# Ten pairs of seven block products in place of nine, and whole sums of h for the early pairs

## The chip, the cores and the metric

The kernel runs on one core of one Trainium2 chip. A core has five engines that run side by side, each through its own list of instructions: TensorE (PE in the profile; PEld is its weight load), VectorE (DVE), ScalarE (ACT), GpSimd (POOL) and SyncE (SP), which here only issues DMAs. They wait for each other through semaphores. The metric is the device time of one execution, in microseconds.

## The reference

The reference is a block-sorted attention followed by a feed-forward layer:

```python
B, H, S, D, n_blocks = 4, 8, 768, 64, 8          # block = 96
P = sinkhorn(sort_net)                            # five rounds of exp and normalising, 8 x 8 per head
k_sorted = einsum('bhij,bhjcd->bhicd', P, k_blocks)
v_sorted = einsum('bhij,bhjcd->bhicd', P, v_blocks)
attn = softmax(q_block @ k_sorted_block.T / sqrt(D))   # inside each block of 96
x = (attn @ v_sorted_block) -> [3072, 512]        # all heads of a token side by side
h = x @ w_in                                      # [3072, 2048]
g = maximum(h, 0) + alpha * minimum(h, 0)
out = g @ w_out                                   # [3072, 512], float32
```

Everything before `out` can be done with matrix products in bf16 and float32 accumulation, and is done so here.

## The kernel before

**Stages.** There are 32 groups of 96 tokens (`attention(g, prio)`, four batches of eight blocks). For every batch k and v are loaded, spread into block form (`conv_k`, `conv_v`, mostly on POOL), multiplied by the sorting matrix on PE (`prep_k`, `prep_v`) and copied out of PSUM. A group then gives scores, softmax and 96 columns of `xT`. The feed-forward layer runs beside the attention of later groups. `ffn1(tok, end, ft, prio)` makes 128 of the 2048 features of `g` for a chunk of 192 or 384 tokens: four matmuls on PE (line 889), a ReLU of the negative on ACT (line 899), and a scalar_tensor_tensor on DVE (line 903) that writes the tile `hT`. In the kernel's own names `hT` is therefore `g`, stored with features on the partitions; the text says h for it. `ffn2(t, prios)` multiplies one tile of 128 tokens by `w_out`: 16 matmuls of 512 columns (line 928), a copy to `outstg` and a store.

**Pairs.** Two neighbouring tiles can be taken together by `strassen(ta, prio)`. The tokens are halved by tile (ta, ta+1), the features by even and odd blocks of 128, the output columns by left and right 256. That is a 2 x 2 block product, and it is made with seven block products in place of eight. Each is eight matmuls of 256 columns (line 1027), added in two halves (hf 0 and 1) as two list entries. Four sums of h are needed (line 1002), n = 1 to 4, where n = 2 reads n = 1, and n = 4 reads n = 2; four of the seven products read a sum of h, the other three read `hT` itself. Before the change each sum is made in two operations of 512 columns (hf 0 covers features 0 to 1023, hf 1 the rest). `snap` copies the running sum in PSUM to SBUF three times a pair (line 414, the tile `sn` or, for every other pair, `KSz`), `total` adds it to a bank (line 1042), `store` sends the tile out. The sums of w_out that the products need are made once for all pairs, by `w_sums` (line 966): eight operations of 1024 columns, into `KS[1]`, `VST[1]` and `WT3`, buffers that hold keys and values of batch 1 and masks until then. The dictionary `PAIRS` names the first tile of each pair and which of two sets of buffers it uses.

**What sets the order.** Every operation is recorded in `_Graph` under a number, in the order in which the program adds it. The string `SEQ` is an order of all of them, written out: a bare number leaves the operation on the first engine that it may use, a letter p, a or d puts it on POOL, ACT or DVE, and an entry such as `i4H` is a run of matmuls that only keep PE busy. Each engine runs its operations in that order and waits (`wait_ge`) for what it depends on; `sums` and `w_sums` may run on DVE (the default) or POOL, copies out of PSUM on ACT (the default) or DVE. Nothing is decided when the kernel runs. All loads are issued by POOL, between its computing operations, and the stores and transposes by SP.

**Rings.** `hT` has room for 1024 tokens. `CHUNKS` says where each chunk of tokens lies, so that a chunk may be overwritten only when the tiles in it have been multiplied by w_out.

Of the kernel before, what the change touches and what calls it, by code (L numbers as in the profile page):

```python
# [48 lines left out]
460 397 474 398d 424 437d 453 475 425 477 462 478 461 516 426d 463 427 428 476 505 517 466 170 454 479 498 455
456d 467d 483 518 506 457 501 499 492 502 458d 465 500 493 464 552 484 510 511 366 503 490 371 513 553 494 512  # L50
514 519 370 373 485 491 507 554 534 515 537 508d 495d 372 369 546 581 535 486d 536 496 367 538 365 497 487 540
539 368 543 488d 555 530 541 582 531 520 544 542 583 521 547 561 647 562d 568 584 545 522d 509 548 651 569 565
570 563 566 572 573 523 549 383 550 571 564 524d 590 574 567 591 648 575 650 578 576 592 525 579 577 594 595
556 593 617 596 655 614 399 597 580 623 557 632 653p 615 558d 559 652 616 624 618 489 633 657p 626 600 560 625
585 619 429 627 634 601 586 599 629 630 628 587d 641 551 642 654 656 631 620 643 588 589 635 598 691 644 692
685 621 645 603 646 663 664 602 604 686 688 693 689 659 605 665d 694 622 700 666 701 687 658 660 708 702 690
720 667 709 703 710 661 459 711 668 712 714 721 713 715 669 704 706 722 670 716 707d 717 718 671d 705 723 737
731 738 749 732 662 719 672 750 740 673 739 741 735 730 636 743 674 675 637 638d 742 751 695 676 696 778 697d
746 677 736 744 758 779 729 678 724 759 745 752 747 748 725 679 766 780 726d 769 760 734 753 767 768 837 770
639 733 698 772 761 781 763 754 788 773 764 771 755d 848 765 775 681 838 776 774 847 762 777 682 853 789 727  # L60
795 613 683 798 787 839 801 846 796 611 799 790d 802 849 756 809 606 797 800 610 810 791 852 811 840 866 782
805 806 812 608 792 867 803 793 684 794 831 832 807 813 833 607 814 609 804 850 834 851 815 612 816 874 868
835 817d 854 818 875 855 783 784d 819 924 841 836 877 876 881 820 878 857 879 869 821 808 822 823 858 925 926
824 934 880 935 859 863 856 888 860 825 842 932 827 828 864 892 865 885 861 933 889p 862 882 829 843d 886 936
887 883 896 937d 927 893p 884 870 897 921 894p 938 680 918 922 898d 871 890 640 939 923 899 872d 952 919 920
895p 900 943 844 901d 940 944 902 941 953 903 891p 928 954 699 945 949 785 904d 942 905 906 929 966p 1002 930d
946 907 1003 950 873 947 728 908 951 931 909 948 910 911 963 960 967p 955 1004 1022 912 964 965 757 961 914
962 1023 999 968p 996 976 915 1000 997 956 786 969p 1001 998 957 1013 970p 916 1024 1010 977 1042 971p 1011
972 1005 974 975 973p 958d 1014 1012 1016 978 830 1015 1019 1025 1017 1043 913 1020 980 979 1006 981 1018 982
1021 1030 1033 1044 1031 986d 1034 983 1007 959 1008d 1026 987 1032 1035 1045 1036 1027 1148p 1028d 826 1037  # L70
1038 1039 1076p 1062 1040 984 1050 1041 1029 1009 1063 1053 1046 988 1077p 1051 1054 985 989 845 1052 1078p
917 1047 1048d 1056 1064 1084 1057 990 1055 1085 1058 1146p 992 1059 1060 1079p 1112 1088 993 1049 1065 1061
1070 994 1071 1073 1074 1072 1086 1075 1087 1113 1106 1089 1107 1109 1090 1110 1080p 1066 1108 991 1111 1092
1093 1114 1150 1120 1121 1094 1122 1115 1081p 1091 1132 1096 1123 1082p 1126 1097 1124 1098 1133 1127 1125
1129 1147p 1128 1134 1099d 995 1095 1154 1140 1083 1155 1130 1067 1100 1102 1141 1103 1131 1152p 1068 1158
1149p 1135 1182 1143 1142 1176 1160 1183 1104 1144 1156 1145 1177 1116 1157 1178 1184 1179 1210 1180 1190 1151
1117 1159 1161 1162 1153p 1191 1181 1163 1069 1193 1192 1185 1118 1196 1194 1136 1166d 1167 1197 1195 1137
1168 1169 1198 1208p 1138d 1199 1202 1200 1164 1201 1119 1165 1205 1203 1204 1238 1216 1217 1206 1207 1239
# [1165 lines left out]
```

## Time and profile before

| | us |
|---|---|
| three runs | 230.91, 234.92, 365.86 |
| their median | 234.92 |
| the execution that was profiled | 230.35 |
| its span, first to last instruction | 228.6 |
| what lies around the span | 1.75 |

The granted clock of TensorE was 1.00 over the whole span. The profile lists for each engine how long it was busy and what it waited for. Busy time of PE is the union of its instructions, and a matmul's record lasts longer than the spacing of two matmuls that follow each other closely, so small gaps between matmuls don't show as idle; the starts in the timeline show them. Numbers such as L1002 are lines of the program; line 414 is the one helper that makes all copies, so its groups are told apart by their tiles.

### The profile page before, as it was taken

Reading aid. Unit: us, or ns where it says so; the run is one execution under the profiler, and the core shown is the slowest. Engines: PE = TensorE matmul, PEld = TensorE weight load, DVE = VectorE, ACT = ScalarE, POOL = GpSimd, SP = SyncE. Lnnn points to the kernel's source line nnn. Section 1 sums busy time; section 2 is a strip of 40 time slices with the busy share of each in tenths; the row PEclk is TensorE's granted clock in tenths of the full one; section 3 lists DMA queues with packets and bytes.
Section 4 is the critical chain, followed back from the end, with each engine's and each line's share of the span. In section 5 each row is a group of like instructions: output and inputs, shape, how many; then the busy total and the mean of one; then the engine's idle time right before and its main releaser. Section 6 shows DMA issues by size and latency. Waiting matters only on the chain.

```text
span 228.6 us, 6971 instructions
## 1 busy us (share of the span) xinstructions
PE 218.5 (96%) x2807; PEld 158.1 (69%) x2807; DVE 192.3 (84%) x419; ACT 160.5 (70%) x448; POOL 152.8 (67%) x182
## 2 busy tenths in 40 slices
PE   3898999999999999999999999999999999999994
PEld 3467588685556656546677877777777777999983
DVE  5669599897898999999999999989878877878584
ACT  4378667889989987778788885567676797554310
POOL 7969129859498995992999999954385712624660
PEclk9999999999999999999999999999999999999999
DMA  5999999995994199679944995477343524040304
GB/s 65 214 214 196 215 206 193 178 178 81 187 214 97 34 152 105 140 77 212 229 91 82 136 124 124 81 100 174 92 118 81 83 52 99 3 126 3 138 3 185
DMA packets 64033, 29.05 MB, mean 127 GB/s; under 512 B 55280, under 2 KB 58880, under 8 KB 64000
## 3 DMA queue, kind: packets, MB, share of 16 engines
q0 software_dynamic: 24816, 13.63, 44.6%
q1 hardware_dynamic: 39184, 14.97, 31.9%
q8 instruction: 22, 0.36, 0.7%
q14 instruction: 11, 0.09, 0.1%
HBM read 27.28 MB, written 6.29 MB: 147 GB/s over the span
## 4 chain that ended last, share of the span: by engine, by line
PE 66%; DVE 10%; DMA 10%; POOL 9%; ACT 2%; issue 1%; POOLq 0%
PE psH L889 29%; PE psYP L1027 19%; DMA KS<-in_k_dram 10%; PE psYP L928 5%; POOL KSz L664 3%; DVE hT L903 3%; PE psS L764 3%; PE psO L818 3%; PE psYP L718 2%; PE psO L1027 2%; DVE xq L831 1%; PE psS L1027 1%; POOL w_in_bf L1105 1%; DVE VST L966 1%; POOL QN L444 1%
## 5 line engine op out<-in xcount | busy, mean ns | idle before, releaser
L889 PE MATMUL psH<-xT,w_in_bf 128*128 128x384 bf16 (+1 forms) x624 | 98.2, 295 | 0.5 <-DVE hT L903 0.3
L903 DVE SCALAR_TENSOR_TENSOR hT<-t,omaT,psH 128x384 bf16<-128x384 f32 (+1 forms) x156 | 79.7, 529 | 16.8 <-ACT t L899 15.7
L899 ACT ACTIVATE t<-psH 128x384 f32<-128x384 f32 x126 | 61.6, 496 | 34.9 <-PE psH L889 32.1
L889 PEld LDWEIGHTS psH<-xT,w_in_bf 128*128 128x128 bf16 x624 | 54.2, 98 | 21.7 <-DVE hT L903 2.3
L798 ACT ACTIVATE Esb<-psS,nf 96x96 bf16<-96x96 f32 x192 | 46.3, 346 | 0.6 <-DVE nf L770 0.6
L414 POOL COPY VDz<-VST 64x384 bf16<-64x384 bf16 x40 | 35.3, 882 | 9.4 <-PE psYP L718 3.7
L664 POOL COPY KSz<-KS 64x512 bf16<-64x512 bf16 x36 | 26.0, 721 | 16.4 <-DMA KS<-in_k_dram 11.9
L928 PE MATMUL psYP<-w_out_bf,hT 128*128 128x512 bf16 x96 | 24.3, 379 | 0.0
L770 DVE TENSOR_REDUCE nf<-psS 96x8 f32<-96x768 f32 x24 | 22.7, 948 | 1.4 <-PE psS L764 1.3
L1002 POOL TENSOR_TENSOR Sm<-hT 128x512 bf16<-128x512 bf16 x11 | 13.2, 1204 | 15.2 <-DVE hT L903 14.7
L444 POOL DMA_DIRECT2D QN<-in_q_dram x24 | 20.1, 844 | 0.0
L831 DVE TENSOR_TENSOR xq<-psO,rec 96x512 bf16<-96x512 f32 x27 | 18.4, 683 | 0.4
L1002 POOL TENSOR_TENSOR VDz<-hT 128x512 bf16<-128x512 bf16 x7 | 8.2, 1170 | 14.6 <-DVE hT L903 14.3
L1027 PE MATMUL psYP<-w_out_bf,hT 128*128 128x256 bf16 x128 | 17.9, 273 | 0.0
L1027 PEld LDWEIGHTS psYP<-w_out_bf,hT 128*128 128x128 bf16 x128 | 12.1, 98 | 2.5
L928 PEld LDWEIGHTS psYP<-w_out_bf,hT 128*128 128x128 bf16 x96 | 8.4, 97 | 7.2
L414 ACT ACTIVATE VS<-psYP 112x512 bf16<-112x512 f32 x17 | 11.8, 692 | 1.8 <-PE psYP L718 1.8
L818 PE MATMUL psO<-VS,ET 112*128 112x65 bf16 x248 | 12.7, 194 | 0.1
L818 PEld LDWEIGHTS psO<-VS,ET 112*128 112x128 bf16 x248 | 10.6, 98 | 1.8 <-DVE xq L831 0.4
L764 PEld LDWEIGHTS psS<-KT,QTz 64*128 64x128 bf16 (+1 forms) x248 | 6.5, 97 | 7.0 <-ACT t L899 2.3
L764 PE MATMUL psS<-KT,QTz 64*128 64x96 bf16 (+1 forms) x248 | 10.8, 206 | 0.4 <-DVE KT L414 0.2
L414 ACT ACTIVATE KT<-psYP 128x512 bf16<-128x512 f32 x15 | 8.9, 597 | 2.9 <-PE psYP L677 2.9
(196 smaller groups left out, 364.0 us busy)
## 6 DMA issues: line engine op xcount, KB each, us to landing
out_dram<-outstg SPq DMA_DIRECT2D x24, 256.0 KB, 2.5
KS<-in_k_dram POOLq DMA_DIRECT2D x3, 768.0 KB, 9.6
QN<-in_q_dram POOLq DMA_DIRECT2D x24, 96.0 KB, 4.5
w_in_bf<-in_moe_w_in_dram POOLq DMA_DIRECT2D x4, 512.0 KB, 18.8
w_out_bf<-in_moe_w_out_dram POOLq DMA_DIRECT2D x2, 1024.0 KB, 19.9
VST<-in_v_dram POOLq DMA_DIRECT2D x4, 384.0 KB, 10.9
hT<-in_q_dram POOLq DMA_DIRECT2D x1, 768.0 KB, 7.3
VST<-in_v_dram POOLq DMA_DIRECT2D x1, 768.0 KB, 13.2
```

Of the source, the lines that this page charges most:

```text
L414: return e.activation(o, i, ACTF.Copy) if e is nc.scalar else e.tensor_copy(o, i)
L444: G.add(POOL, lambda e, h=h: e.dma_start(AP(QN, h % 4 * 128 + h // 4 * 64, [[3072, 128], [512, 6], [1, 64]]), AP(q.tensor, b * HB + h * S ...
L664: G.add(POOL, lambda e, hp=hp: e.tensor_copy(AP(KSz, hp * 64 * 3072 + u % 3 * 1024 + hp * 64, [[3072, 64], [128, 8], [1, 64]]), AP(KS[n], ...
L764: inst = e.matmul(o, AP(QTz[n], hp * 64 * 3072 + h4 * 768 + i * 96, [[3072, 64], [1, w]]), AP(KT[n], hp * 64 * ld + (h4 * 8 + i) * bk, [[l ...
L770: G.add(DVE, lambda e: e.tensor_reduce(AP(nx, 0, [[8, 96], [4, 2], [1, 4]]), AP(psX, 0, [[1024, 96], [512, 2], [96, 4], [1, 96]]), AxisLis ...
L798: inst = e.activation(AP(Esb[me], p * 128, [[1024, 96], [64, 2], [1, 48]]), AP(psX, (p // 4) * 512 + (p % 4) * 96, [[1024, 96], [48, 2], [ ...
L818: inst = e.matmul(AP(psZ, hp * 512 + h4 * 68, [[1024, 128], [1, 65]]), AP(ET[me] if far else ET[m], pos(h4, hp) * 96, [[800, nk], [1, 128] ...
L889: inst = e.matmul(AP(pt, poff + x * n, [[1024, 128], [1, n]]), AP(w_in_bf, kt * DFF + (ft + x) * 128, [[KT_TILES * DFF, 128], [1, 128]]), ...
L899: G.add(ACT, lambda e: e.activation(AP(t1, tb, [[1152, 128], [1, k * n]]), AP(pt, poff, [[1024, 128], [1, k * n]]), ACTF.Relu, scale=-1.0) ...
L903: G.add(DVE, lambda e, x=x: e.scalar_tensor_tensor(out=AP(hT, (ft + x) * RING + place(tok), [[FT_TILES * RING, 128], [1, n]]), in0=AP(t1, ...
L928: inst = e.matmul(AP(bank[0], bank[1], [[1024, 128], [1, n]]), AP(hT, ft * RING + place(tok), [[FT_TILES * RING, 128], [1, 128]]), AP(w_ou ...
L1027: inst = e.matmul(AP(pt, po + off, [[1024, 128], [1, 256]]), sa, mb, start=begin and j == 0, stop=j == 7, skip_group_check=True)
```

## The change

There are three parts.

- In `strassen`, pairs whose first tile is below 20 take each sum of h in one operation over all 1024 columns (eight feature blocks of 128 in place of four), and it waits for all 16 feature blocks of `hT`. Pairs 20 and 22 keep two operations of 512.
- `PAIRS` gets the entry `4: 0`: tiles 4 and 5, until now two calls of `ffn2`, become a tenth pair. Since `w_sums` is called ahead of the first pair, its operations are recorded ahead of pair 4.
- `SEQ` is another order from its 372nd entry on (about 60 us into the span). The numbers shift as well, since 14 fewer operations are recorded (1348 for 1362).

```diff
@@ -42,48 +42,47 @@
 270 264d 279 299 286 284 165 267 287 265 300 162 266d 277 273 289 280 274d 306 288 334 166 275 335 301 276 293
...
-344d 357 329 358 349 388 377 408 319 389 390 409 411 391 249 330 168 412 410 392 413 347 414 415 331 348d 351
-352 649 332 416 417 420 346d 418 526 527 438 421 350d 353 164p 533 439 360 361 419 532 354d 528 441 400 440
...
+344d 357 329 358 349 388 377 408 319 389 390 409 411 391 249 330 168 412 410 392 413 347 526 393 414 348d 331
+415 350d 351 420 532 346d 416 417 169 352 332 418 421 438 419 360 529 439 353 440 354d 422 441 546p 548 442
...
@@ -391,7 +390,7 @@
...
-    PAIRS = {6: 0, 8: 0, 10: 0, 12: 1, 14: 0, 16: 1, 18: 0, 20: 1, 22: 0}
+    PAIRS = {4: 0, 6: 0, 8: 0, 10: 0, 12: 1, 14: 0, 16: 1, 18: 0, 20: 1, 22: 0}
...
@@ -985,22 +984,27 @@
         def hk(t, odd, hf):
             return [("hT", 8 * hf + 2 * j + odd, y) for j in range(4) for y in gr[t]]
 
+        whole = ta < 20
+        nj = 8 if whole else 4
+
         def blk(t, odd, hf):
-            return AP(hT, (8 * hf + odd) * RING + (ra, rb)[t], [[FT_TILES * RING, 128], [2 * RING, 4], [1, 128]])
+            return AP(hT, (8 * hf + odd) * RING + (ra, rb)[t], [[FT_TILES * RING, 128], [2 * RING, nj], [1, 128]])
 
         def sv(n, hf):
-            return AP(st, (n - 1) * 1024 + hf * 512, [[ld, 128], [128, 4], [1, 128]])
-        for hf in range(2):
+            return AP(st, (n - 1) * 1024 + hf * 512, [[ld, 128], [128, nj], [1, 128]])
+        for hf in range(1 if whole else 2):
+            hfs = (0, 1) if whole else (hf,)
             for n, x, y, op in ((1, (1, 0), (1, 1), AluOpType.add), (2, 1, (0, 0), AluOpType.subtract),
                                 (3, (0, 0), (1, 0), AluOpType.subtract), (4, (0, 1), 2, AluOpType.subtract)):
                 r = []
                 for v in (x, y):
-                    r += [("S", m, v, hf)] if isinstance(v, int) else hk(*v, hf)
+                    for z in hfs:
+                        r += [("S", m, v, z)] if isinstance(v, int) else hk(*v, z)
...
-                G.add(SMALL, f, {"dve": 520, "pool": 1180}, r=r, w=[("S", m, n, hf)] + first, prio=prio + n / 100)
+                G.add(SMALL, f, {"dve": 90 * nj, "pool": 270 * nj}, r=r, w=[("S", m, n, z) for z in hfs] + first, prio=prio + n / 100)
```

Read through the numbering of operations, the new lists place the 48 sums of h as follows. On DVE: 20 whole ones and 9 halves. On POOL: 12 whole ones and 7 halves. The old lists had 33 halves on DVE and 39 on POOL. Of the eight sums of w_out two are now on POOL (one before). Of the copies of `VS` out of PSUM 3 go from DVE to ACT, of those of `KT` one.

More of the change, by code (lines that the diff above doesn't have):

```diff
@@ L49 @@
[L49 to L78, printed above, removed]
@@ new lines @@
+803 840 804 639 858 811 837 812 817 813 856 841 873 838 818 846 839 857 814 819 859 792 880 793 820 634 821
+822 881 823d 636 638 884 860 874 824 794d 825 847 842 637 635 861 885 640 926 882 826 863 827 690 828 927 862
+864 575 829 830 865 831 869 875 883 894 848 866 886 833 834 928 934 870 871 867 891 868 935 694 887 888 929
+849d 835 892 889 876 938 893 939 898 899 890 936 937 900d 877 662 895 923 940 738 924 941 920 901 896p 902 954
+921 925 945 795 709 878d 922 942 946 903d 943 955 947 904 905 956 930 906d 951 907 908 944 1000 948 952 931
@@ new lines @@
+932d 909 1001 910 911 912 796 953 913 949 850 897 950 879 1002 965 962 1020 966 974 933 963 914 957 967 964
+997 994 1003 916 998 836 1021 995 851 999 917 1022 958 996 1011 918 832 959 1008 968p 975 1009 1012 969 1040
+970 972 767 960 973 1010 1014 1023 1013 971 976 1017 1015 1004 1041 977 1018 1016 978 979 1042 980 1019 1028
+1031 961 1029 1060 1032 981 1005 1006d 984d 1030 1033 1024 1061 1034 1035 1037 1025 1043 982 985 919 1038 1036
+986 1062 1007 1039 983 1051 1052 1026d 1027 987d 988 1048 1053 1044 1045 1063 990 991 1049 1057 1050 1054
@@ new lines @@
+1046d 1106 1078 992 1058 1059 1071 1055 1056 1047 1072 1068 1080 1107 1079 1069 1073 1108 1070 1082d 1064 1074
+1081 1100 1083 1103 1075 1101 1104 1126 1102 1086 1084 1114 1115 1105 993 1117 1118 1065 1116 1085 1087 1090
+1076p 1120 1119 1109 1121 1123 915 1091 1124 1066d 1127 1088 1110 1142p 1089 1122 1111 1077p 1125 1128 1092
+1093d 1134 1094 1137 1135 1172 1136 1096 1138 1166 1139 1140p 1173 1167 1097 1168 1141p 1169 1170 1067 1174
+1129 1144 1145 1098 1148d 1171 1146 1180 1147 1112d 1113 989 1183 1150 1181 1182 1184 1151 1185 1156d 1186
@@ L87 @@
+1213 1302 1270 1273 1299 1300 1303 1301 1201p 1261p 1306 1304 1328 1334 1218 1271 1305 1307 1308 1310 1309
+1165 1311 1259 1320 1263 1276 1312 1318 1314 1315 1316 1220 1277 1319 1221 1317 1274 1313 1326 1322 1327 1330
+1222 1335 1278 1332 1275 1279 1323 1280 1333 1338d 1336 1329 1223 1282 1324p 1339 1340 1337 1341 1219 1283
+1321p 1342 1284 1343 1266 1267 1269 1344 1325p 1345 1331 1281 1346 1285 1347
 """.split()
```

30 lines of the change are left out of this document (20 added, 10 removed).

## The prediction

> **What bounds the kernel now.** I read the busy times first, then a table of four stages.
>
> ```profile
> PE 218.5 (96%) x2807; PEld 158.1 (69%) x2807; DVE 192.3 (84%) x419; ACT 160.5 (70%) x448; POOL 152.8 (67%) x182
> ...
> 0.00:55.00 55.00, 48.80 (x1053) 36.16 (x1054) 43.47 (x125) 38.58 (x76) 38.14 (x58) 1.00 1.15 174
> 55.00:105.00 50.00, 49.54 (x521) 28.96 (x520) 45.59 (x80) 41.94 (x124) 41.23 (x51) 1.00 0.92 131
> 105.00:215.00 110.00, 109.78 (x1142) 84.07 (x1141) 94.89 (x196) 78.61 (x246) 68.56 (x70) 1.00 0.59 106
> 215.00:228.60 13.60, 10.38 (x98) 8.95 (x95) 8.33 (x19) 1.37 (x3) 4.85 (x5) 1.00 0.26 98
> ```
>
> The columns of the table are the stretch, its length, then busy time and instructions of PE, PEld, DVE, ACT, POOL, then granted clock and DMA. From 55 to 215 us PE is idle for 0.7 us of 160. It is the bound wherever the change acts; the first 55 us run by the part of the lists that stays as it is. The view of waits agrees. PE's longest wait is at the start, and behind the start nothing holds it for more than half a microsecond in total:
>
> ```profile
> PE psYP L1201 <- ACT identb L414: 3.1, 1, 3.1
> ...
> PE psYP L677 <- POOL KSz L664: 0.5, 2, 0.3
> ```
>
> Busy time hides small gaps, because the record of a matmul overlaps the next one. So I took prices from starts in the timeline of PE (start, duration, instruction):
>
> ```profile
> 67.63 0.41 PE L818 MATMUL psO<-VS,ET 112*128 112x65 bf16 x8
> 67.87 1.03 PE L928 MATMUL psYP<-w_out_bf,hT 128*128 128x512 bf16 x4
> 68.74 0.40 PE L718 MATMUL psYP<-BDV,VDz 128*128 128x64 bf16 x8
> 68.97 0.81 PE L889 MATMUL psH<-xT,w_in_bf 128*128 128x384 bf16 x4
> 69.62 0.34 PE L853 MATMUL psO<-identb,xq 96*128 96x96 bf16 x4
> 69.79 1.03 PE L928 MATMUL psYP<-w_out_bf,hT 128*128 128x512 bf16 x4
> 70.75 0.34 PE L764 MATMUL psS<-KT,QTz 64*128 64x96 bf16 x8
> 71.03 0.82 PE L889 MATMUL psH<-xT,w_in_bf 128*128 128x384 bf16 x4
> ```
>
> Start to start, four matmuls of 512 columns take 0.87 us, four of 384 take 0.65, eight of the attention 0.23 to 0.28, four transposes 0.17. The stretch 55 to 105 holds these:
>
> ```profile
> L889 PE MATMUL psH<-xT,w_in_bf 128*128 128x384 bf16 x128 | 25.0, 326 | 0.2
> L928 PE MATMUL psYP<-w_out_bf,hT 128*128 128x512 bf16 x80 | 20.2, 379 | 0.0
> L718 PE MATMUL psYP<-BDV,VDz 128*128 128x64 bf16 x96 | 4.8, 193 | 0.0
> L818 PE MATMUL psO<-VS,ET 112*128 112x65 bf16 x64 | 3.3, 194 | 0.0
> L764 PE MATMUL psS<-KT,QTz 64*128 64x96 bf16 x62 | 2.7, 205 | 0.0
> L853 PE MATMUL psO<-identb,xq 96*128 96x96 bf16 x32 | 2.7, 206 | 0.0
> L677 PE MATMUL psYP<-BDM,KSz 128*128 128x64 bf16 x48 | 2.4, 193 | 0.2 <-POOL KSz L664 0.2
> L764 PE MATMUL psS<-KT,QTz 64*96 64x96 bf16 x10 | 0.6, 212 | 0.0
> ```
>
> 32 x 0.65 + 20 x 0.87 + 18 x 0.23 + 8 x 0.24 + 9 x 0.28 + 8 x 0.17 = 48.1 us of 50. Gaps of 1.9 us in this stretch are therefore the most that a better order could win there, apart from less work.
>
> **Part one, tiles 4 and 5 as a pair.** Removed from PE are 2 x 16 matmuls of 512 columns: 8 groups of four at 0.87 = 6.96 us. Added are 7 x 8 of 256 columns. Their price is in the chain of waits:
>
> ```profile
> 134.17 1.75 PE psYP L1027 x16
> ```
>
> 1.75 / 16 = 0.109 us, times 56 = 6.13 us. PE gains 0.83 us, and as PE is the bound, I count all of it. The pair puts work on other engines: four sums, three snaps, three totals, less two copies to the staging tile.
>
> **Part two, whole sums.** The durations of the halves, by engine (12 groups, 33 on DVE and 39 on POOL; here the first of each engine), and of the nearest operations of 1024 columns, the sums of w_out:
>
> ```profile
> L1002 DVE TENSOR_TENSOR Sm<-hT x13: 366/418/581, 94.9 to 219.8; 128x512 bf16<-128x512 bf16 x13
> L1002 POOL TENSOR_TENSOR Sm<-hT x11: 1152/1157/1479, 98.1 to 218.0; 128x512 bf16<-128x512 bf16 x11
> ...
> L966 DVE TENSOR_TENSOR WT<-w_out_bf x2: 681/682/682, 60.8 to 93.6; 128x1024 bf16<-128x1024 bf16 x2
> L966 DVE TENSOR_TENSOR VST<-w_out_bf,KS x2: 677/1344/2010, 91.1 to 96.6; 128x1024 bf16<-128x1024 bf16 x2
> L966 POOL TENSOR_TENSOR KS<-w_out_bf,VST x1: 2118/2118/2118, 95.9 to 95.9; 128x1024 bf16<-128x1024 bf16 x1
> ```
>
> A whole sum is between 0.68 us and two halves, 0.84, on DVE; I take 0.68, the row of its own size. On POOL it is between 2.12 and 2.31; I take 2.12 for the same reason. Undisturbed, sums on POOL go from 39 x 1.157 = 45.1 us to 12 x 2.12 + 7 x 1.157 = 33.5, and on DVE from 33 x 0.418 = 13.8 to 20 x 0.68 + 9 x 0.418 = 17.4. The other operations that the lists move are priced by these rows:
>
> ```profile
> L1042 DVE TENSOR_TENSOR outstg<-psYP,sn 128x256 f32<-128x256 f32 x10 | 4.1, 414 | 0.6 <-PE psYP L1027 0.6
> L1042 DVE TENSOR_TENSOR outstg<-psYP,sn 128x512 f32<-128x512 f32 x5 | 3.4, 670 | 0.7 <-PE psYP L1027 0.7
> L414 DVE COPY sn<-psYP 128x256 f32<-128x256 f32 x8 | 3.4, 420 | 0.6 <-PE psYP L1027 0.6
> L414 DVE CAST VS<-psYP 112x512 bf16<-112x512 f32 x9 | 6.2, 685 | 0.0
> L414 ACT ACTIVATE VS<-psYP 112x512 bf16<-112x512 f32 x17 | 11.8, 692 | 1.8 <-PE psYP L718 1.8
> ```
>
> DVE gets 3.6 for sums, 1.5 for totals and 0.4 for one snap; it loses three copies of VS, one of KT and one output copy (0.69 each) and a sum of w_out (0.68), 4.1 together: 193.7 us, 1.4 more. ACT gets the four copies (2.8 by its own row) and two snaps for one output copy: about 163.5. POOL loses 11.6 and gets one sum of w_out: 143.3. None of them exceeds PE's load, so on the average all of it lies beside PE, and POOL's relief is worth nothing by itself. The cover is thinnest in 55:105, where DVE already has 45.6 of 50 us; there it gets the pair's four sums, totals and two snaps (5.0) and gives back four copies out of PSUM (2.8), the w_out sum, and the two halves of pair 6 that start before 105 (0.8). That is 46.3 of the 49.2 that remain, so PE still covers it. If the cover fails, each further microsecond of DVE is one of the kernel; that is the second rival.
>
> Waiting for all 16 feature blocks in place of eight makes a sum start later. Queued behind a waiting sum on DVE are the `hT` writes that free PE's banks for `ffn1`. In the new lists the sums stand behind the last `ffn1` of their chunk, and PE gets the products that read `hT` itself first; I cost this at nothing, and its bounds are the gaps: 0 to a few tenths for each of eight pairs, at most 2.
>
> **Part three, the order.** The sums of w_out move from 88 to 102 us down to some 63 to 95, and one of them, on POOL (2.1), is put ahead of `conv_v` of batch 2. POOL is idle for 8.8 of 50 us in the table's second stretch, so this fits, and the loads of batch 3 behind it on its queue should start at about the same place. The cost is taken as zero, between the 1.9 that could be won and the same lost. At the end:
>
> ```profile
> 216.25 0.66 PE psH L889 x8
> ...
> 224.73 0.89 PE psO L1027 x8
> ```
>
> Behind the last `ffn1` matmul (216.91) stood 19 half products, 8.3 of the 8.7 us until 225.6. In the new list 22 stand there, so PE has more to do while the last sums are made, and only their order changes.
>
> **Sum.** 228.6 - 0.83 = 227.8 of span, with the 1.75 around it 229.5 us. It is made against the profiled execution (230.35), which agrees with the fastest run (230.91). The median of the runs shown, 234.92, lies 4.6 above the profiled time and was not explained by any row.
>
> **Rivals.** First, the new order also closes gaps. For it speaks that gaps of 1.9 us exist in 55:105, and that copies out of PSUM, for which PE's next work waits, go from DVE to ACT; against it, that DVE gets no lighter there. At most 1.9 beside the 0.83, and an allowance of 1.0 for the gaps behind 105, which I did not count: 230.35 - 3.7 = 226.6 us.
>
> Second, slower: DVE and POOL hold each other up, and DVE becomes the bound. The timeline of the last sums shows how:
>
> ```profile
> 219.99 2.56 POOL L1002 TENSOR_TENSOR Sm<-hT,Sm 128x512 bf16<-128x512 bf16 x2 [0.88 <-DVE Sm L1002]
> 220.17 1.37 DVE L1002 TENSOR_TENSOR VDz<-hT,VDz 128x512 bf16<-128x512 bf16 x1
> ```
>
> The other long sums on DVE are these:
>
> ```profile
> L1002 DVE TENSOR_TENSOR Sm<-Sm,hT x6: 411/421/824, 102.3 to 219.5; 128x512 bf16<-128x512 bf16 x6
> L1002 DVE TENSOR_TENSOR VDz<-hT x5: 412/417/932, 155.7 to 207.2; 128x512 bf16<-128x512 bf16 x5
> ```
>
> A DVE sum of 0.42 us begun just after a POOL sum took 1.37, until that one had ended; the w_out sum of 2.01 us above lay beside POOL's of 2.12 in the same way. The Trainium skill states the rule ("SBUF — State Buffer", section "SBUF: two separate sides"): a DVE operation with two SBUF inputs and a GpSimd operation that reads SBUF take one pair of ports in turn, whichever is first for its whole instruction. Both rows agree with it. By that rule, an operation twice as long holds the other twice as long, and this speaks against whole sums. In the old run the longest of each group cost DVE (1.37 - 0.42) + (2.01 - 0.68) + (0.82 - 0.42) + (0.93 - 0.42) + (0.58 - 0.42) = 3.4 us. Doubled, that is 3.4 us more; it decides from about 2.9 us on (46.3 + 2.9 fills 49.2). If all of the holds fall where DVE is full and PE waits out each one, the time is 229.5 + 3.4 = 232.9 us. Against it: the lists leave half as many sums on POOL, and in 55:130 nearly none.
>
> Third, the pair gives PE nothing, because the 0.83 us turn into gaps ahead of products that wait for sums: 230.4 us.
>
> **Numbers.** Forecast 0.60 (its own range 228.8 to 230.2); gaps closed 0.15; DVE bound 0.15; nothing gained 0.10. The range goes down to 227.2, most of the way to the first rival, and up to 234.2, which takes in the second rival and a forecast that stands as far above its profile as the median of the runs shown does (234.92 - 0.83 = 234.1). About 2% (4.6 us) is what a measurement of this kernel can tell from no change. Faster by more than that (below 225.7) needs more than all gaps: 0.05. Slower (above 235) needs DVE's holds and a further loss, such as the loads of batch 3 starting late: 0.07. Within: 0.88.
>
> **What would show it.** Right: 64 matmuls of 512 columns for w_out in place of 96, 560 of 256 columns in place of 504, PE's busy time down by about 0.8, whole sums of 0.68 us on DVE and 2.1 on POOL, and PE idle for under 1 us from 55 to 215. Wrong on the gaps: prices and counts of the same stretch of PE come to over 49 of 50 us. Wrong on DVE: sums of 1.5 us and more between 60 and 130, DVE above 48 of 50, and PE waiting for a product's sum. It would also be wrong if the wait of POOL for batch 3's values grew well beyond what it is now.

## The result, and the profile after

The change makes the kernel slower: 237.32 us at the median against 231.5 (the median of six executions of the old kernel, in place of the three known before), a ratio of 1.0264 with a 95% interval of 1.0227 to 1.0301. The ratio leaves out the executions that lie over 1.5% above the fastest of their kernel: 239.59 us of the new, 234.92 and 365.86 us of the old. The execution that was profiled took 235.75 us with a span of 233.9, against 230.35 and 228.6: 5.3 us more of span.

The busy times of the new kernel, in the first part of its page:

```profile
PE 218.5 (93%) x2831; PEld 160.5 (69%) x2831; DVE 198.8 (85%) x413; ACT 162.4 (69%) x446; POOL 143.0 (61%) x163
```

PE is busy for as long as before, and the span is longer, so the 5.3 us are idle time of PE. The table of stretches says where. Its columns are those of the table in the prediction (stretch, length, then PE, PEld, DVE, ACT, POOL, clock, DMA). After:

```profile
55.00:105.00 50.00, 48.31 (x538) 30.66 (x536) 45.51 (x82) 43.65 (x128) 42.85 (x52) 1.00 0.85 122
105.00:170.00 65.00, 64.32 (x700) 46.97 (x699) 60.36 (x111) 52.29 (x166) 34.35 (x39) 1.00 0.88 132
170.00:180.00 10.00, 7.40 (x71) 4.70 (x68) 9.70 (x12) 4.66 (x14) 4.57 (x2) 1.00 0.43 104
180.00:210.00 30.00, 29.83 (x284) 24.30 (x285) 24.01 (x51) 17.12 (x51) 13.89 (x7) 1.00 0.31 68
210.00:220.00 10.00, 9.07 (x96) 8.32 (x95) 7.82 (x17) 3.67 (x9) 5.64 (x4) 1.00 0.04 13
```

Before, two of the same places (105 to 215 together and 55 to 105 stand in the prediction):

```profile
170.00:180.00 10.00, 10.00 (x93) 7.00 (x91) 7.46 (x13) 6.29 (x19) 6.56 (x6) 1.00 0.49 91
210.00:220.00 10.00, 10.00 (x104) 9.31 (x102) 6.75 (x19) 3.60 (x9) 4.62 (x5) 1.00 0.22 80
```

From 170 to 180 PE loses 2.60 us, from 210 to 220 0.93, and from 55 to 105 1.23 more than before (1.69 for 0.46). That is 4.8 us; the stretches from 105 to 170 (0.68 idle for 0.22) and from 180 to 210 (0.17 for none) add 0.6. From 220 us to the end PE is idle for 3.2 us in both kernels. From 170 to 180 DVE is at 9.70 of 10 with only 12 instructions. The view of waits of the new kernel, for PE (total, times, longest):

```profile
PE psH L888 <- DVE hT L902: 1.7, 4, 0.9
PE psYP L1031 <- DVE Sm L1006: 1.6, 1, 1.6
PE psYP L1031 <- DVE outstg L1046: 1.2, 1, 1.2
...
PE psYP L717 <- POOL VDz L413: 1.0, 1, 1.0
```

The lines have shifted: L888 is `ffn1`, L902 the write of `hT`, L1006 a sum of h, L1031 a block product, L1046 a total, L413 the helper of copies, L717 the product with the values, L965 a sum of w_out. Before, PE's wait for `hT` came to 0.3 us, and the others shown are not in that view.

**175 to 180 us.** The timeline of the new kernel (start, duration, instruction, and in brackets the idle time before it and what ended it):

```profile
174.92 2.12 POOL L1006 TENSOR_TENSOR Sm<-hT 128x1024 bf16<-128x1024 bf16 x1 [18.26 <-DVE hT L902]
...
175.09 2.50 DVE L1006 TENSOR_TENSOR Sm<-hT 128x1024 bf16<-128x1024 bf16 x1
...
177.12 2.44 POOL L1006 TENSOR_TENSOR VDz<-hT 128x1024 bf16<-128x1024 bf16 x1
177.51 0.41 DVE L1046 TENSOR_TENSOR outstg<-psYP,sn 128x256 f32<-128x256 f32 x1
177.84 2.27 DVE L1006 TENSOR_TENSOR Sm<-Sm,hT 128x1024 bf16<-128x1024 bf16 x1
177.98 0.61 PE L1031 MATMUL psYP<-KS,hT 128*128 128x256 bf16 x4 [1.19 <-DVE outstg L1046]
180.03 1.13 DVE L902 SCALAR_TENSOR_TENSOR hT<-t,omaT,psH 128x384 bf16<-128x384 f32 x2
180.17 0.61 PE L1031 MATMUL psYP<-VST,Sm 128*128 128x256 bf16 x4 [1.58 <-DVE Sm L1006]
```

POOL begins a sum at 174.92. DVE's sum of two tiles begins at 175.09, 0.17 us behind it, and ends at 177.59, 0.55 us after POOL's (177.04). Its undisturbed time is 0.68, so it stood still for about 1.8 us. The total queued behind it on DVE, which frees the bank that PE's next product needs, comes at 177.51. Then it happens again: POOL begins at 177.12, and DVE's next sum, begun at 177.84, takes 2.27. The total itself, which reads PSUM and one tile in SBUF, took its usual 0.41 beside POOL's sum. The bracket of the first line says how the two came to begin together: POOL had waited 18.26 us for a write of `hT`, and DVE, which makes these writes, reaches its own sum of the same pair right behind it (after one copy). In the old kernel's timeline the same stretch has POOL sums of half the size, six in a row from 174.06 to 181.4 us, and beside the first five a single DVE sum:

```profile
175.29 1.16 POOL L1002 TENSOR_TENSOR Sm<-Sm,hT 128x512 bf16<-128x512 bf16 x1
176.14 0.59 DVE L1002 TENSOR_TENSOR VDz<-hT 128x512 bf16<-128x512 bf16 x1
```

That one met POOL's too, but only the last 0.31 us of it, and cost DVE 0.17 (0.59 for 0.42).

**213 us.** One of the last `ffn1` groups waits in the same way, as the writes of `hT` that free its banks are queued on DVE behind a held sum:

```profile
213.00 2.12 POOL L1006 TENSOR_TENSOR Sm<-hT,Sm 128x1024 bf16<-128x1024 bf16 x1
...
213.32 2.07 DVE L1006 TENSOR_TENSOR VDz<-hT 128x512 bf16<-128x512 bf16 x1
...
215.32 1.38 DVE L902 SCALAR_TENSOR_TENSOR hT<-t,omaT,psH 128x192 bf16<-128x192 f32 x4
216.10 0.83 PE L888 MATMUL psH<-xT,w_in_bf 128*128 128x192 bf16 x8 [0.93 <-DVE hT L902]
```

**83 us.** This one is no sum. POOL's queue now has two conversions of keys and the product of a mask (L623) ahead of the last conversion of values of batch 2, and PE's product with these values waits:

```profile
78.31 2.25 POOL L663 COPY KSz<-KS 64x512 bf16<-64x512 bf16 x2
80.62 1.77 POOL L413 COPY VDz<-VST 64x384 bf16<-64x384 bf16 x2
82.47 0.95 POOL L623 TENSOR_TENSOR BDV<-mkhV,dsel 128x64 bf16<-128x64 f32 x1
83.49 0.82 POOL L413 COPY VDz<-VST 64x384 bf16<-64x384 bf16 x1
...
84.45 0.39 PE L717 MATMUL psYP<-BDV,VDz 128*128 128x64 bf16 x8 [1.00 <-POOL VDz L413]
```

The waits of 1.6, 1.2, 0.9 and 1.0 us at these three places add up to 4.7 us; the span grew by 5.3.

### The profile page after: what moved, and what is told of

Its sections match the earlier page's. It is cut to its first block, busy times and chain, and to the rows that moved or that the text cites. A ratio compares the mean times of both kernels' runs of the same rounds, so it can differ in the third digit from the quotient of the medians.

```text
span 233.9 us, 6983 instructions
## 1 busy us (share of the span) xinstructions
PE 218.5 (93%) x2831; PEld 160.5 (69%) x2831; DVE 198.8 (85%) x413; ACT 162.4 (69%) x446; POOL 143.0 (61%) x163
## 4 chain that ended last, share of the span: by engine, by line
PE 56%; POOL 19%; DMA 15%; DVE 5%; issue 2%; ACT 2%; POOLq 0%; DVEq 0%
PE psH L888 25%; PE psYP L1031 20%; DMA KS<-in_k_dram 13%; POOL VDz L413 7%; POOL KSz L663 5%; PE psO L1031 2%; PE psO L817 2%; PE psS L763 2%; DVE Sm L1006 2%; DMA ET<-Esb 2%; PE psS L1031 1%; DVE hT L902 1%; PE psYP L717 1%; PE psYP L676 1%; POOL w_in_bf L1109 1%
## 5 line engine op out<-in xcount | busy, mean ns | idle before, releaser
L888 PE MATMUL psH<-xT,w_in_bf 128*128 128x384 bf16 (+1 forms) x624 | 97.7, 295 | 1.7 <-DVE hT L902 1.7
L902 DVE SCALAR_TENSOR_TENSOR hT<-t,omaT,psH 128x384 bf16<-128x384 f32 (+1 forms) x156 | 79.5, 528 | 13.8 <-ACT t L898 12.0
L888 PEld LDWEIGHTS psH<-xT,w_in_bf 128*128 128x128 bf16 x624 | 54.2, 98 | 22.2 <-DVE hT L902 3.2
L797 ACT ACTIVATE Esb<-psS,nf 96x96 bf16<-96x96 f32 x192 | 46.3, 345 | 0.3 <-DVE nf L769 0.3
L413 POOL COPY VDz<-VST 64x384 bf16<-64x384 bf16 x40 | 36.1, 902 | 7.0 <-PE psYP L717 2.9
L663 POOL COPY KSz<-KS 64x512 bf16<-64x512 bf16 x36 | 23.6, 657 | 14.2 <-DMA KS<-in_k_dram 11.9
L1006 POOL TENSOR_TENSOR Sm<-hT 128x1024 bf16<-128x1024 bf16 (+1 forms) x5 | 10.1, 2022 | 34.2 <-DVE hT L902 34.1
L1006 POOL TENSOR_TENSOR VDz<-hT 128x1024 bf16<-128x1024 bf16 (+1 forms) x6 | 10.1, 1690 | 20.0 <-DVE hT L902 19.7
L1031 PE MATMUL psYP<-w_out_bf,hT 128*128 128x256 bf16 x144 | 20.0, 273 | 0.0
L830 DVE TENSOR_TENSOR xq<-psO,rec 96x512 bf16<-96x512 f32 x28 | 19.1, 681 | 0.4
L927 PE MATMUL psYP<-w_out_bf,hT 128*128 128x512 bf16 x64 | 16.1, 379 | 0.0
L1031 PEld LDWEIGHTS psYP<-w_out_bf,hT 128*128 128x128 bf16 x144 | 13.3, 98 | 2.9 <-ACT sn L413 0.2
L413 ACT ACTIVATE VS<-psYP 112x512 bf16<-112x512 f32 x20 | 13.9, 695 | 1.2 <-PE psYP L717 0.9
L717 PEld LDWEIGHTS psYP<-BDV,VDz 128*128 128x128 bf16 x192 | 8.2, 98 | 4.3 <-ACT t L898 1.4
L413 ACT ACTIVATE KT<-psYP 128x512 bf16<-128x512 f32 x16 | 9.5, 597 | 2.0 <-PE psYP L676 1.9
```

Source lines behind the costliest of these rows:

```text
L413: return e.activation(o, i, ACTF.Copy) if e is nc.scalar else e.tensor_copy(o, i)
L663: G.add(POOL, lambda e, hp=hp: e.tensor_copy(AP(KSz, hp * 64 * 3072 + u % 3 * 1024 + hp * 64, [[3072, 64], [128, 8], [1, 64]]), AP(KS[n], ...
L797: inst = e.activation(AP(Esb[me], p * 128, [[1024, 96], [64, 2], [1, 48]]), AP(psX, (p // 4) * 512 + (p % 4) * 96, [[1024, 96], [48, 2], [ ...
L888: inst = e.matmul(AP(pt, poff + x * n, [[1024, 128], [1, n]]), AP(w_in_bf, kt * DFF + (ft + x) * 128, [[KT_TILES * DFF, 128], [1, 128]]), ...
L902: G.add(DVE, lambda e, x=x: e.scalar_tensor_tensor(out=AP(hT, (ft + x) * RING + place(tok), [[FT_TILES * RING, 128], [1, n]]), in0=AP(t1, ...
L1006: return e.tensor_tensor(out=sv(n, hf), in0=i[0], in1=i[1], op=op)
```

## The experiments

The theory after this reading, **holds**: the second rival of the prediction at places that the prediction had not named. A POOL sum that begins first stops a DVE operation with two inputs in SBUF until it ends, and PE waits for what is queued behind. The rivals: **order**, the new list is laid out worse for POOL and DVE whatever their sums do; **size**, an operation of 1024 columns is the cause wherever it stands; and **pair**, the tenth pair costs more than it saves. All runs below were compared with the old kernel on the same chip (medians of 231.17 to 231.28 us). Diffs of the list show the moved entries between their neighbours, with `...` for what lies between; the text says what the entries are.

### Taking the meetings apart

In the first kernel the sum of w_out that the change put on POOL ahead of the values of batch 2 goes to DVE.

```diff
-422 441 546p 548 442
+422 441 546 548 442
```

> The changed kernel with one edit: the w_out sum n = 1, hf 0, goes from POOL back to DVE at the same place of the list. Theory 'POOL order': that 2.3 us operation delays POOL's conversions of batch 2 until PE waits 1.0 us for one of them at 84 us; the gap goes, and the span falls by about 1.0 to 1.2 us, to some 232.8. Theory 'DVE load' (DVE, busy 198.8 us, is simply too full): DVE gets 0.7 us more, the gap at 84 moves to another product, and the time stays or rises by up to 0.7. Theory 'holds only' (all of the loss is at 175 and 213 us): no change beyond 0.3 us.

238.52 us, 1.0314 [1.0269, 1.0359]: slower yet. The wait at 83 us stayed (1.0 us, now at 84), for POOL used the free time to wait for the load of the values:

```profile
64.89 14.06 POOL L413 COPY VDz<-VST 64x384 bf16<-64x384 bf16 x13 [2.78 <-DMA VST<-in_v_dram]
```

So that sum of w_out is not what delays the values, and the gain of 1.0 to 1.2 us expected for it did not come. A new loss came at 140 us, where the new kernel had none:

```profile
138.53 2.12 POOL L1006 TENSOR_TENSOR Sm<-hT 128x1024 bf16<-128x1024 bf16 x1
138.98 2.21 DVE L1006 TENSOR_TENSOR Sm<-hT 128x1024 bf16<-128x1024 bf16 x1
```

In the new kernel DVE began this sum at 138.06, 0.28 us ahead of POOL (138.34), and took 0.74; POOL took 2.44. Here POOL began 0.45 us ahead, and PE waited 1.1 us. Nothing at this place had been edited. Between the medians (238.52 for 237.32) that is about the whole difference; the profiled execution, the slowest of the four with 239.48, also ran at half clock for a while, which the end of this document takes up.

In the second kernel, pair 14's third sum (1076) goes from POOL to DVE, between the first and the second, and pair 16's third (1142), also on POOL, behind pair 14's fourth. The sums are as large and as many; only the two meetings at 175 and 177 us are gone.

```diff
-1064 1074 1081 ... 1090 1076p 1120 ... 1110 1142p 1089 ... 1111 1077p 1125
+1064 1074 1076 1081 ... 1090 1120 ... 1110 1089 ... 1111 1077p 1142p 1125
```

> The changed kernel with one edit at 175 us: the sum n = 3 of pair 14 goes from POOL to DVE, between n = 1 and n = 2, and POOL's n = 3 of pair 16 goes behind n = 4 of pair 14. So POOL runs nothing beside DVE's sums n = 1 and n = 2 of pair 14. Theory 'holds': these two take 0.68 us in place of 2.50 and 2.27, PE's gaps of 1.2 and 1.6 us there go, and the span falls by 2.5 to 3.0 us, to some 231.2. Theory 'DVE load': DVE has 0.68 us more in a stretch where it is busy for 9.7 of 10 us, so PE's gaps stay at 2.5 us or more and the span stays at 233.5 to 234.6.

233.38 us, 1.0099 [1.0084, 1.0114]. The sums that had taken 2.50 and 2.27 us now take 0.68 or less each:

```profile
175.53 1.28 DVE L1006 TENSOR_TENSOR Sm<-hT 128x1024 bf16<-128x1024 bf16 x2
...
177.07 0.68 DVE L1006 TENSOR_TENSOR Sm<-Sm,hT 128x1024 bf16<-128x1024 bf16 x1
```

POOL's next sum begins at 177.83, when they have ended. The stretches of this kernel:

```profile
170.00:180.00 10.00, 10.00 (x91) 6.54 (x89) 8.90 (x19) 5.39 (x17) 2.12 (x1) 1.00 0.42 103
210.00:220.00 10.00, 9.08 (x96) 8.28 (x95) 8.47 (x20) 3.76 (x9) 4.09 (x4) 1.00 0.01 2
```

Two entries give back 3.9 of 5.8 us of the medians, and 2.3 us of span between the profiled executions (231.6 for 233.9; *holds* expected 2.5 to 3.0, a DVE that is simply too full at most 0.4). The medians differ by more because the clock stays up as well: the mean granted clock is 0.999 or 1.000 in all four executions. PE is full from 170 to 180, with DVE at 8.90 of 10 in place of 9.70, while DVE has 19 instructions in place of 12: it does more and is busy for less. This is what *holds* says. *Size* alone and *pair* would have left the loss in place. At 210 to 220 nothing was edited and nothing changed.

In the third, all 32 whole sums are on DVE (the letter p of twelve entries is taken away; five of them are shown).

```diff
-576 671p 700 ... 1008 968p 975 ... 1090 1076p 1120 ... 1160 1198p 1099 ... 1301 1201p 1261p
+576 671 700 ... 1008 968 975 ... 1090 1076 1120 ... 1160 1198 1099 ... 1301 1201 1261p
```

> The changed kernel with all 32 whole sums on DVE at their places in the list (12 come from POOL). DVE gets 12 x 0.68 = 8.2 us and loses the holds of its sums (2.50 + 2.27 + 2.07 + 1.53 in place of 0.68 + 0.68 + 0.42 + 0.68, 5.9 us). Theory 'holds': PE's gaps at 175 to 180 and at 215 go (3.9 us in all), span about 230. Theory 'DVE load': DVE's sum of work rises above 200 us, its queue is late in more places, span 234 to 238.

235.2 us, 1.0168 [1.0146, 1.0191]. The meetings at 175 are gone, and PE is full from 170 to 180, but DVE now has too much to do behind 180 us, and PE waits there:

```profile
180.00:195.00 15.00, 13.83 (x114) 9.38 (x112) 13.24 (x25) 9.00 (x27) 0.00 (x0) 1.00 0.21 48
```

PE loses 1.2 us of 15 from 180 to 195. It also waits 1.0 us for converted values at 84 us, as in the changed kernel, and 1.0 us for converted keys at 46 us, where the lists are still those of the old kernel. The span is 233.7 us, where *holds* alone expected about 230 and a DVE that is simply too full 234 to 238; DVE is busy for 200.5 us. So once no meeting is left, DVE's load does count in this list: twelve sums moved give back less than the two entries of the second kernel.

The fourth joins the first two edits and puts pair 18's fourth sum (1201), the one of 213 us, on DVE.

```diff
-1301 1201p 1261p
+1301 1201 1261p
```

> The two edits of the first two runs together, and the whole sum n = 4 of pair 18 moved from POOL to DVE (it holds a DVE sum of pair 20 for 1.65 us at 213, and PE then waits 1.1 us). Theory 'POOL order' and 'holds' together: the span falls by 1.1 + 2.8 + 1.1 = 5.0 us to some 229, level with the kernel before or up to 0.8 us under it if the pair's saving is real; measured time about 230 to 231. Theory 'DVE load': 233 or more. If the pair costs more than it saves, the span stays 1 us or more above that of before even with these gaps gone.

234.17 us, 1.0136 [1.0116, 1.0156]. The loss at 213 us is gone, as *holds* says. The wait at 84 (1.0) and the meeting at 140 us of the first kernel (1.1) are both there, which makes it slower than the second alone. The span of 229 us that was expected from the sum of the three did not come (232.7): the edits don't add up, for an edit can shift POOL and DVE against each other behind it, as at 140 us.

### The other places

From here on the edits of the second kernel and the one of 213 us are kept. In this one a conversion of keys (528), one more (527) and the mask product (164p) go behind the conversion of values that PE waited for at 83 us.

```diff
-428 528 170 ... 498 527 499 ... 551 164p 500 ... 580 460 458
+428 170 ... 498 499 ... 551 500 ... 580 460 528 527 164p 458
```

> The changed kernel with three edits of the list: pair 14's n = 3 on DVE with POOL's n = 3 of pair 16 behind n = 4 of pair 14 (as in the second run), pair 18's n = 4 on DVE, and POOL's two key conversions and one small mask product of batches 2 and 3 moved behind the last value conversion of batch 2, which is what PE waits for at 84 us. Theory 'holds and POOL order': the span falls from 231.6 (second run) by 1.1 at 213 us and by 1.1 at 84 us, to 229.4, within 1 us of the kernel before. Theory 'POOL is simply behind from its load of values': the gap at 84 us stays at 1 us or moves to the first key product, span 230.5. Theory 'DVE load': the edit for pair 18 brings nothing, span 231 or more.

233.41 us, 1.01 [1.0054, 1.0146]; the four executions spread from 232.67 to 234.22. The wait at 83 us is gone, so it was the order of POOL's queue. But the span of 229.4 us that was expected did not come (232.2). PE now waits 0.5 us for converted keys at 93 us, and two meetings cost it 0.9 us at 99 and 1.1 at 140. The second is that of the first experiment; the first is between two sums of w_out:

```profile
96.71 2.11 POOL L965 TENSOR_TENSOR KS<-w_out_bf,VST 128x1024 bf16<-128x1024 bf16 x1
97.23 2.15 DVE L965 TENSOR_TENSOR VST<-w_out_bf,VST 128x1024 bf16<-128x1024 bf16 x1
```

The next moves one conversion of keys (528) in place of two, and takes the two meetings apart: the sum of w_out (552) and pair 12's first sum (968) go to DVE.

```diff
-498 499 ... 460 528 527 164p 458 ... 588 553 645 ... 652 552p 615d ... 1008 968p 975
+498 527 499 ... 460 528 164p 458 ... 588 553 552 645 ... 652 615d ... 1008 968 975
```

> The changed kernel with every meeting of a POOL sum and a DVE sum taken out that was seen to make PE wait: pair 14's n = 3 and pair 18's n = 4 on DVE, pair 16's n = 3 behind n = 4 of pair 14 (as in the eighth run), and also pair 12's n = 1 and both halves of the fourth w_out sum on DVE; of POOL's work ahead of the last value conversion of batch 2 only one key conversion and the mask product are moved behind it. Theory 'holds': against the run with three places (span 232.2) PE's gaps of 1.3 us at 140, of about 0.6 of the 1.0 at 99 and of 0.5 at 93 go, span 229.8, which is within 0.5 us of the kernel before in the same session (229.5). Theory 'the new order is slow for other reasons': 231.5 or more.

232.4 us, 1.0052 [1.0025, 1.0078]: the fastest form of the change, and still slower than the old kernel by 1.2 us. The losses at 83, 99, 140, 175 and 213 us are gone; seven entries of some 1350 give back 4.9 of 5.8 us. For the wait at 83 us it was *order* that was right, for the others *holds*. What is left at single places behind 65 us is a wait of 0.7 us for converted keys at 93 us and one of 0.4 for a transpose at 121.5. The span is 230.7 us, between the 229.8 that *holds* expected and the 231.5 of its rival, and 2.1 us above the old kernel's profile. Of these, 0.7 us arise ahead of 56 us, where the lists are the same (a group of `ffn2` begins at 56.12 for 55.43 us), so this one profile does not say what the difference of the medians is made of.

The last kernel takes these two. Three of the eight loads of q that POOL issues ahead of the conversions of keys (368, 369, 372) go behind the third of them, with them the first transpose of q (383), and on PE one attention product (763) goes behind the `ffn1` group (782) that followed it.

```diff
-559 368 610 ... 531 369 597 ... 589 372 562 ... 591 383 600 ... 533 584 ... 854 763 782 764
+559 610 ... 531 597 ... 589 562 ... 591 600 ... 533 368 369 372 383 584 ... 854 782 763 764
```

> Keeps all three parts and the moves of the kernel without meetings, and takes two of its three remaining gaps: the last three of the eight loads of q for batch 2 go on POOL behind three conversions of keys (the PE gap of 0.82 us at 93 us stood behind 6.7 us of load issues), and on PE one second attention product goes behind the ffn1 group that followed it (the gap of 0.59 us at 121.5 us stood for its transpose). Theory of the order (what is left of the loss is the places of single entries): both gaps close, the time falls by 1.0 to 1.4 us from that of the kernel without meetings, to a ratio of 0.999 to 1.001, so that the pair's gain is all that is left to win. Rival (what is left is the weight of the new work itself, spread over many small waits): the gaps open at the next products and the ratio stays at 1.004 to 1.006.

234.47 us, 1.0139 [1.0114, 1.0164]: slower by 2 us. Both gaps closed, and two larger ones opened, one of 1.6 us for a transpose at 97 us, the other here:

```profile
102.77 2.11 POOL L477 DMA_DIRECT2D VST<-in_v_dram  x4 [6.37 <-DMA QTz<-QN]
...
107.12 2.11 POOL L1006 TENSOR_TENSOR Sm<-hT 128x1024 bf16<-128x1024 bf16 x1
...
107.73 2.05 DVE L1006 TENSOR_TENSOR Sm<-hT 128x1024 bf16<-128x1024 bf16 x1
...
110.17 1.05 PE L1031 MATMUL psYP<-w_out_bf,hT 128*128 128x256 bf16 x8 [0.91 <-DVE outstg L1046]
```

The later loads of q make the transposes of q late. POOL then waits 6.37 us for these before it issues the loads of values, and so begins the next pair's sum at 107.12 in place of 104.67 us, 0.61 ahead of one of DVE's: a meeting where there had been none (that sum of DVE had taken 0.68), caused by entries some 15 us ahead of it. The expectation of 1.0 to 1.4 us less was wrong, and its rival named neither of these places; that the last 1.2 us are in the places of single entries is not shown.

### The parts of the change alone

Two kernels leave tiles 4 and 5 as calls of `ffn2`, everything else as in the two kernels above that they answer to (three places, and no meetings).

```diff
-    PAIRS = {4: 0, 6: 0, 8: 0, 10: 0, 12: 1, 14: 0, 16: 1, 18: 0, 20: 1, 22: 0}
+    PAIRS = {6: 0, 8: 0, 10: 0, 12: 1, 14: 0, 16: 1, 18: 0, 20: 1, 22: 0}
```

> The kernel of the run before with pair 4 taken away alone: tiles 4 and 5 again by 16 matmuls of 512 columns each, in the places of the pair's products, its sums, snaps and totals left out, all else in the same order. Theory 'the pair saves its matmuls': PE has 0.83 us more to do, and the span is 0.6 to 0.9 us longer than that of the run before. Theory 'the pair costs more than it saves' (its 5 us of DVE work between 80 and 110 us open gaps on PE): the span is the same or up to 1.5 us shorter.

> The kernel of the run before without pair 4 (tiles 4 and 5 by 512-column matmuls in the places of the pair's products). Theory 'the pair saves its matmuls': 0.6 to 0.9 us longer than the run before, since no gap hides it now. Theory 'the pair costs more than it saves': the same or shorter by up to 0.9 us, as in the earlier pair of runs (231.3 without, 232.2 with).

The first took 232.91 us, 1.0063 [1.0042, 1.0085], less than the 233.41 of its counterpart with the pair. But in it DVE began the sum at 139 us ahead of POOL (139.24 and 139.52), so that the wait of 1.1 us at 140 was missing; it doesn't measure the pair. The second has a counterpart without meetings: 232.89, 1.0072 [1.0052, 1.0092], for 232.40 with the pair. With the pair it is 0.5 us less between the medians and 0.6 of span (231.3 for 230.7); the forecast was 0.83. The intervals overlap, so the size of this saving is not shown. PE's idle time behind 55 us is about the same in the two (5.0 us with the pair, 5.2 without), though not at the same places: without the pair PE waits 0.8 us for a write of `hT` at 107 us. *Pair* falls: in the one comparison without meetings the pair costs no time.

The next undoes the whole sums alone. In the new order each is two halves again, one behind the other on the same engine.

```diff
-        whole = ta < 20
+        whole = False
```

> The changed kernel with whole sums undone alone: every sum is again two operations of 512 columns, one right behind the other at the same place and on the same engine; pair 4 and the order stay (the second halves of pair 12 stand behind its first ones). Theory 'holds come from the two engines meeting, not from the size': four DVE halves meet four POOL halves of 1.16 us at 175 us, each waits for one, and their end is nearly as late as with whole sums; only the first half products can start 1.2 us sooner; PE's gap there is 1.5 to 2.5 us in place of 3.0 and the span 232 to 233.5. Theory 'size of the operation': each half is held for at most 0.95 us as in the kernel before, gaps under 0.7, span 230 to 231.

236.85 us, 1.0238 [1.0188, 1.0288], not told apart from the change itself (1.0264 [1.0227, 1.0301]), but for other reasons in part. Two waits of PE, with the chain behind the first:

```profile
160.55 1.15 POOL L1008 TENSOR_TENSOR VDz<-hT 128x512 bf16<-128x512 bf16 x1 [15.25 <-DVE VDz L1008]
161.73 0.42 DVE L1008 TENSOR_TENSOR VDz<-VDz,hT 128x512 bf16<-128x512 bf16 x1 [1.26 <-POOL VDz L1008]
163.55 0.72 PE L1033 MATMUL psYP<-VST,VDz 128*128 128x256 bf16 x5 [1.84 <-ACT KSz L415]
...
180.66 0.61 PE L1033 MATMUL psYP<-KS,hT 128*128 128x256 bf16 x4 [1.25 <-DVE outstg L1048]
```

The first, of 1.8 us at 163, is no meeting. All sums of pair 12 are recorded as writers of the same buffer (`first` in `strassen`) and so run one after another; POOL's second half had to wait for DVE's halves, and DVE then for it. Without this wait the span of 234.7 us would be some 232.9 (an estimate, by taking off the 1.84). At 175 to 182 us, where the halves do meet, PE waits 1.25, 0.35 and 0.25 us, 1.9 in all for 2.8 with whole sums: within the 1.5 to 2.5 that was expected of meetings, and not under 0.7. At 213 us there is no wait. So *size* is not the cause by itself, since the engines meet in this order with halves too, but it sets what a meeting costs.

The other way round, whole sums on the old order, with nine pairs: each whole sum stands where the later half stood, on that half's engine, and in a second kernel on DVE throughout.

```diff
-    PAIRS = {4: 0, 6: 0, ...
+    PAIRS = {6: 0, ...
```

> The kernel before with whole sums alone: pairs as before (nine), the old order, each whole sum of pairs 6 to 18 in the place and on the engine of its later half; five operations that read a sum earlier wait behind it. Theory 'whole sums cost by themselves': POOL holds DVE for up to 2.1 us wherever they meet, and products start later; span 1 to 3 us above 228.6. Theory 'the loss is of the new order': 228.3 to 229.3.

> The old order with nine pairs and whole sums, as in the run of 241.2 us, but with all whole sums on DVE. In that run PE waited 4.0 us for whole sums of POOL and 2.8 us for those of DVE, and the clock was at half for 3.4 us. Theory 'whole sums cost through POOL' (2.1 us of one operation, in chains of three, and holds): without POOL the waits fall under 1.5 us, no clock drop, span 229.5 to 232. Theory 'waiting for all 16 feature blocks costs': the products still wait wherever they did, span 236 or more.

243.31 us, 1.0519 [1.0471, 1.0567], and 240.93, 1.0433 [1.0392, 1.0474]. PE's waits, of the first and of the second:

```profile
PE psYP L1031 <- POOL Sm L1006: 4.0, 2, 2.5
...
PE psYP L1031 <- DVE Sm L1006: 2.8, 2, 1.6
```

```profile
PE psYP L1030 <- DVE Sm L1005: 5.1, 4, 1.6
```

The first, with a span of 241.2 us, is far above what either theory expected (at most 231.6). Without any whole sum on POOL the loss is still 9.7 us, and the span of 239.5 is what waiting for all 16 feature blocks was expected to bring (236 or more). Whole sums on DVE have medians of 0.68 to 0.69 us in that kernel, so few were held; they come late. Each needs all 16 feature blocks, where the first halves could begin with eight, and each stands where the later half stood; the two are not told apart here. So whole sums on the old order cost more than the whole change does, and what makes them bearable is the new order, which brings the meetings.

## Why the prediction was wrong

The forecast was 229.5 us, and the range ended at 234.2; the median is 237.32, the profiled execution 235.75.

**Right.** PE is the bound, and what it can't cover costs a microsecond for each. The counts and prices held:

```profile
L927 PE MATMUL psYP<-w_out_bf,hT 128*128 128x512 bf16 x64 | 16.1, 379 | 0.0
...
L1006 DVE TENSOR_TENSOR Sm<-hT,Sm x4: 677/678/1343, 103.4 to 151.0; 128x1024 bf16<-128x1024 bf16 x4
```

A whole sum takes 0.68 us on DVE when nothing holds it and 2.12 on POOL (the sum at 174.92). ACT is at 162.4 (163.5 forecast) and POOL at 143.0 (143.3). The pair's 0.83 us came out as 0.5 to 0.6, within the noise. PE's busy time did not fall by the 0.8 that the prediction asked for, but the records of matmuls overlap, and a change this small can't be read from them.

**The term that was mis-sized: DVE.** 193.7 us was forecast, 198.8 came. One group of its sums, with a mean of 1022 ns in place of 680:

```profile
L1006 DVE TENSOR_TENSOR Sm<-hT 128x1024 bf16<-128x1024 bf16 x8 | 8.2, 1022 | 0.0
```

The sums of h on DVE were priced at 20 x 0.68 + 9 x 0.418 = 17.4 us; all their groups together took 25.0. The sums of w_out took 5.1 for 6 x 0.68 = 4.1. That is 8.6 us of holding against the 3.4 that the prediction counted in the old trace: 5.2 more, and 5.1 is what DVE's total was off by. The second rival doubled each old hold and came to 3.4 more, which was too little as well, because whole sums also meet where halves had passed each other. Nor is it sums alone that hold: the longest in the row of four above, 1.34 us at 112.01, had no sum of POOL beside it but a run of conversions of values. And a hold is not yet a loss. The three at 175 and 213 us are 5.1 of the 8.6 us and made PE wait 3.7; the other 3.5 us of holding cost PE little.

**The step that failed: "That is 46.3 of the 49.2 that remain, so PE still covers it".** The figure was sound (45.51 measured). The inference wasn't. It asks whether DVE's load in a stretch of 50 us leaves room on the average, and from that it sized the second rival and put it into 55 to 130 us, where DVE was fullest. The loss came at 175 and 213 us, where DVE had been at 7.46 and 6.75 of 10. A stop of 1.8 us had no cover at a place where PE's next product or bank hung on DVE's next entry, though DVE had been idle for a quarter of that stretch before. "Against it: the lists leave half as many sums on POOL, and in 55:130 nearly none" was true, and looked away from 170 to 220 us, where nine of POOL's twelve whole sums stand. The two lists had been there to be laid side by side: a POOL sum next to a DVE sum for the same pair at 175, with PE's product next in line.

The mechanism itself was the second rival's. The Trainium skill's rule on it ("SBUF — State Buffer", section "SBUF: two separate sides"), that of the two operations the first to start keeps the port pair for its whole instruction, agrees with the meetings of sums shown here, in both directions: DVE 2.50 us beside POOL's 2.12 where POOL began first, and POOL 2.44 beside DVE's 0.74 where DVE did.

**"The cost is taken as zero, between the 1.9 that could be won and the same lost" (part three).** The order cost 1.0 us at 83 us. "POOL is idle for 8.8 of 50 us … so this fits" was the same kind of average. The sum of w_out named there did no harm (the first experiment); conversions of keys and a mask product ahead of the values did, which the prediction had not looked for in the list; one conversion and the mask product moved were enough to end the wait (the kernel of 232.4 us).

**"I cost this at nothing, and its bounds are the gaps" (waiting for all 16 feature blocks).** In the new order PE's long waits are not for a DVE sum that itself waited for `hT`. But the waiting had a part at 175 us: POOL had waited 18.26 us for an `hT` write that DVE's sum also stood behind, and so the two met. On the old order whole sums lose 9.7 us even with all of them on DVE, and 5.1 us of PE's waits there are for sums.

The forecast was made against the profiled execution, and it is this one that stands 1.55 above the range; the other 1.6 us to the median go with the clock (below). What stays open is the last 1.2 us of the best form, and how much of the old order's loss with whole sums is the waiting for all 16 blocks. No form that was run beats the old kernel.

## What to carry to other kernels

When two engines exclude each other for an instruction, don't compare their loads: write down, for each long operation on the one, which operation the other has next in its list, and what PE waits for behind that. Where it must be close, give the short operation the earlier place by more than the tenths by which the lists drift: here an edit some 15 us ahead decided which began first. An average of busy time says that work fits into a stretch; it says nothing of a wait at one point in it.
